# Last rows of a routed mixture of experts: three more blocks of 512 rows, then units of 384, 256 and 128

## The chip, the cores and the metric

The kernel runs on one core of one Trainium2 chip. The metric is the device time of one execution in microseconds (us); the number compared is the median of several executions. One execution is also taken with the hardware profiler, and every row shown below comes from that one. TensorE is called PE, VectorE DVE, ScalarE ACT, GpSimd POOL and SyncE SP; PEld is the loading of weights into PE, and "SPq" or "POOLq" is the sequencer of an engine.

## The reference

A Fourier filter along the sequence gives 19,968 rows of 256 numbers. A gate picks two of eight experts for each row, and the output of a row is the weighted sum of its two experts.

```python
X = np.fft.rfft(x, axis=1)                       # x: 8 x 2496 x 256
x = np.fft.irfft(X * F, n=2496, axis=1).reshape(19968, 256)
noisy = x @ w_gate + np.log1p(np.exp(x @ w_noise)) * noise
top2 = np.argpartition(-noisy, 2, axis=1)[:, :2]  # two of 8 experts
top2_w = softmax over the two
for e in range(8):
    for k in range(2):
        mask = top2[:, k] == e
        h = np.maximum(x[mask] @ w1[e], 0.0)      # 256 -> 1024
        out[mask] += top2_w[mask, k, None] * (h @ w2[e])   # 1024 -> 256
```

So 39,936 rows go through an expert, about 4,990 per expert; which ones is known only once the gate has run.

## The kernel before

The filter is made batch by batch (eight batches), and its matmuls stand among those of the experts. After each batch the gate counts the rows of each expert, writes their numbers into lists in device memory (`route`), and `slots` cuts what has come together into pieces of one size: it makes a small table `tabi` with, for each slot, the place of its list and its expert. The number of slots of a size is fixed when the program is built, since the data can't leave fewer rows than a certain sum: 18 blocks of 512 rows in the first three batches, 23 pairs of two blocks after that, and, when the eighth batch is in, `SINGLE` = 7 single blocks of 512. Then come the remains, `ENDS`: 14 units of 256 rows and 4 of 128. Should the data need more of these (up to 17 and 8), a part behind an `If` at the very end does them one by one. `slots` is called after the last batch for pairs, singles, 256 and 128, in this order; each call is a chain of small DVE instructions with two small matmuls (`sl`, `st`) between them.

All units run through `expert`. A unit of n tiles of 128 rows is handled as follows:

- `read_list` loads its list of row numbers (SP) and turns them into integers (`ids`, POOL).
- `gather` fetches n tiles of rows with indirect DMAs from POOL into the staging slots `xg`, of which there are four of one tile each.
- `turn` brings the rows into the form that PE needs. Blocks of 512 are transposed by DMA (`xt`). Smaller units are copied by POOL (two copies, `kc` = 0 and 1, line 1104 before and 1123 after), transposed by PE (`xps`, one transpose for each tile and kc) and split into a high and a low part (`mxh`, `mxl`).
- `front` loads the two weights of the expert (1 MB each) and splits them, for each unit anew (ACT and DVE, lines 1162 and 1163).
- First layer: 48 matmuls that stream the unit's rows, 128 n columns each (`hps`, lines 123 to 125), into eight results that ACT and DVE take to SBUF (`hh`, `hl`).
- Second layer: for each tile eight pairs of one matmul with 512 columns and one with 256 (`yps`, lines 1235 and 1236). ACT and DVE scale the tile (lines 1240 and 1242), and POOL adds it to the output with an indirect DMA (line 1243, `out<-stage,ids`).

While a unit is in its second layer, the next one has been turned and its first layer is under way. `fetch` sends off the gather of a coming unit; `expert` calls it before the first layer, when

```python
if not self.ahead or self.ahead[0][3] or sum(len(a[2][0]) for a in self.ahead) < 4:
    self.fetch(may)
```

that is, when nothing is waiting, when what waits is turned already, or when fewer than four tiles wait, and again after `front`. Each engine runs its instructions in the order in which the scheduler put them. The tables that say whether the `If` is needed are read into registers of all engines (line 1290): on SP soon after they are made, on the other engines at the end of their work.

## Time and profile before

| | us |
|---|---|
| median of 3 runs (2224.51 to 2234.17) | 2231.22 |
| the profiled execution | 2228.77 |
| its span in the trace | 2227.0 |

The rest of the profiled execution, 1.77 us, lies around the span. In the span PE is busy 98%, DVE 72%, ACT 54% and POOL 45%. By stages: the last single block of 512 rows ends with the DVE instruction at 2015.52 us, the fourteen units of 256 rows follow until about 2183 us, and the four units of 128 rows end at 2217.22 us; the rest of the span is the way of the last tile to device memory and the end of the program. A row of the trace gives a start and a duration; PE's durations overlap, since matmuls are pipelined, so the cost of a matmul is read as the distance between the starts of two of them.

### The profile page before, as it was taken

To read this page: it belongs to the slowest core of one execution; us is meant where nothing else is said; L and a number is where in the kernel's file an instruction comes from. 1 tells how busy PE (TensorE), PEld (TensorE's weight loads), DVE (VectorE), ACT (ScalarE), POOL (GpSimd) and SP (SyncE) were. 2 spreads that over 40 slices of the span, in tenths; PEclk is the share of its full clock that TensorE was granted. 3 is DMA by queue.
4 is the path that set the end of the run, shared out by engine and by line. 5 is a ranking of instruction groups with operands and counts; after the bars stand their busy time and mean duration, and the time that the engine had idled before them with its cause. 6 is when DMAs were issued, how large, how long until landed. Compare 5 with 4: busy or idle time off the path is not lost.

```text
span 2227.0 us, 39429 instructions
## 1 busy us (share of the span) xinstructions
PE 2192.6 (98%) x12687; PEld 1850.7 (83%) x12687; DVE 1613.4 (72%) x3464; ACT 1210.7 (54%) x2373; POOL 1004.9 (45%) x866
## 2 busy tenths in 40 slices
PE   8999999999999999999999999999999999999998
PEld 6668888988888888888888888888888888889997
DVE  4777788869877977787658876696555556567886
ACT  6475655665665455545545454444444444456775
POOL 4035345244433643443444434454545454456663
PEclk9999999999999999999999999999999999999999
DMA  8778879787877767577655767556655556777874
GB/s 248 228 208 220 202 169 213 191 203 174 212 184 176 166 156 178 128 168 167 138 121 129 159 165 138 101 125 125 117 114 120 126 118 140 159 183 222 229 213 123
DMA packets 435434, 370.58 MB, mean 166 GB/s; under 512 B 185643, under 2 KB 345363, under 8 KB 435219
## 3 DMA queue, kind: packets, MB, share of 16 engines
q1 hardware_dynamic: 373907, 283.58, 47.4%
q0 software_dynamic: 61312, 84.40, 23.0%
q8 instruction: 102, 1.67, 0.3%
q14 instruction: 113, 0.93, 0.1%
HBM read 227.73 MB, written 105.25 MB: 150 GB/s over the span
## 4 chain that ended last, share of the span: by engine, by line
PE 93%; DVE 3%; DMA 2%; ACT 1%; issue 1%; SPq 0%; POOL 0%; POOLq 0%; DVEq 0%; ACTq 0%
PE yps L1235 20%; PE hps L123 13%; PE hps L124 13%; PE hps L125 13%; PE yps L1236 10%; PE q L448 3%; PE yps L125 3%; PE yps L124 3%; PE yps L123 3%; PE q L532 2%; DMA stage<-w 1%; PE q L556 1%; PE u L484 1%; PE q L557 1%; PE q L558 1%
## 5 line engine op out<-in xcount | busy, mean ns | idle before, releaser
L1243 POOL DMA_INDIRECT out<-stage,ids x316 | 533.0, 1687 | 363.4 <-DVE stage L1242 199.1
L1235 PE MATMUL yps<-w,hh 128*128 128x512 f32 x1952 | 687.4, 397 | 0.2 <-DVE stage L1242 0.2
L1052 POOL DMA_INDIRECT stage<-y,ids x316 | 343.2, 1086 | 492.3 <-DMA xt<-stage 389.0
L124 PE MATMUL hps<-mxl,w1h 128*128 128x512 f32 (+2 forms) x1424 | 531.3, 374 | 0.3 <-DVE mxl L1116 0.3
L125 PE MATMUL hps<-mxh,w1l 128*128 128x512 f32 (+2 forms) x1424 | 526.3, 371 | 0.0
L1236 PE MATMUL yps<-w,hl 128*128 128x256 f32 x1952 | 520.4, 282 | 0.4 <-DVE hl L1207 0.4
L123 PE MATMUL hps<-mxh,w1h 128*128 128x512 f32 (+2 forms) x1424 | 520.2, 377 | 0.5 <-DVE hl L1207 0.4
L1207 DVE SCALAR_TENSOR_TENSOR hl<-hps,hh 128x512 fp32r<-128x512 f32 (+2 forms) x712 | 433.6, 623 | 90.4 <-ACT hh L1206 88.9
L1206 ACT ACTIVATE hh<-hps 128x512 fp32r<-128x512 f32 (+2 forms) x712 | 379.8, 553 | 196.3 <-PE hps L125 183.7
L1235 PEld LDWEIGHTS yps<-w,hh 128*128 128x128 f32 x1952 | 356.7, 188 | 72.8 <-DVE stage L1242 0.6
L1236 PEld LDWEIGHTS yps<-w,hl 128*128 128x128 f32 x1952 | 367.2, 188 | 27.9 <-DVE hl L1207 1.2
L1240 ACT ACTIVATE stage<-yps,gt 128x256 f32<-128x256 f32 x316 | 142.4, 478 | 366.8 <-PE yps L1236 204.0
L125 PEld LDWEIGHTS hps<-mxh,w1l 128*128 128x128 f32 x1424 | 268.6, 189 | 48.0
L124 PEld LDWEIGHTS hps<-mxl,w1h 128*128 128x128 f32 x1424 | 268.8, 189 | 41.2 <-DVE mxl L1116 1.0
L123 PEld LDWEIGHTS hps<-mxh,w1h 128*128 128x128 f32 x1424 | 264.1, 189 | 43.3 <-DVE hl L1207 3.5
L1242 DVE SCALAR_TENSOR_TENSOR stage<-yps,gt,stage 128x256 f32<-128x256 f32 x244 | 111.9, 479 | 238.0 <-ACT stage L1240 237.7
L1162 ACT CAST w1h<-stage 128x512 fp32r<-128x512 f32 x192 | 119.2, 622 | 120.1 <-DMA stage<-w 59.9
L125 PE MATMUL yps<-w,hl 128*128 128x256 f32 x576 | 159.9, 287 | 2.8 <-DVE hl L1207 2.7
L123 PE MATMUL yps<-w,hh 128*128 128x256 f32 x576 | 161.8, 285 | 0.0
L124 PE MATMUL yps<-w,hh 128*128 128x256 f32 x576 | 161.7, 285 | 0.0
L1163 DVE TENSOR_TENSOR w1l<-stage,w1h 128x512 fp32r<-128x512 f32 x192 | 130.9, 685 | 39.3 <-ACT w1h L1162 38.0
L1163 DVE TENSOR_TENSOR w<-stage,w 128x512 fp32r<-128x512 f32 x228 | 152.5, 683 | 4.8 <-ACT w L1162 4.5
(234 smaller groups left out, 3070.7 us busy)
## 6 DMA issues: line engine op xcount, KB each, us to landing
stage<-w SPq DMA_DIRECT2D x420, 256.0 KB
x<-x SPq DMA_DIRECT2D x88, 256.0 KB
wb<-w SPq DMA_DIRECT2D x18, 1024.0 KB
fx<-fd SPq DMA_DIRECT2D x140, 128.0 KB
fd<-c SPq DMA_DIRECT2D x73, 240.0 KB
out<-z SPq DMA_DIRECT2D x24, 702.0 KB
y<-yt SPq DMA_DIRECT2D x40, 248.6 KB
y<-yt SPq DMA_DIRECT2D x40, 234.0 KB
```

Source lines behind the costliest of these rows:

```text
L123: nc.tensor.matmul(o, lh, rh, start=start, stop=False)
L124: nc.tensor.matmul(o, lh, rl, start=False, stop=False)
L125: return nc.tensor.matmul(o, ll, rh, start=False, stop=stop)
L1052: self.pin(lambda: nc.gpsimd.indirect_dma_start(out=x.bitcast(I32), out_offset=None, in_=self.y[:BLK + ready * ROWS], in_offset=bass.Indir ...
L1162: nc.scalar.copy(h, sv)
L1163: nc.vector.tensor_sub(l, sv, f32v(h))
L1206: r = nc.scalar.activation(h, p, AF.Relu)
L1207: v = nc.vector.scalar_tensor_tensor(l, p, 0.0, f32v(h), op0=ALU.max, op1=ALU.subtract)
L1235: nc.tensor.matmul(bank, h, hl, start=(f == 0), stop=False)
L1236: self.mm = nc.tensor.matmul(p, l, hl[:, 0], start=False, stop=(f == 7))
L1240: nc.scalar.activation(o, p, AF.Copy, scale=gate[:, t])
L1243: a = nc.gpsimd.indirect_dma_start(out=self.io["out"][:BLK + ready * ROWS], out_offset=bass.IndirectOffsetOnAxis(ap=ids[:, t:t + 1], axis= ...
```

## The change

The remains are cut in another way. `SINGLE` is raised by 3, to 10, and a single block may now be filled up: `slots` adds up to 127 rows before it counts. Behind the blocks an expert may have up to seven tiles of 128 left. An odd number of three or more gives one unit of 384 rows (`3 * ROW`) and the rest in units of 256; a single tile gives a unit of 128. `ENDS` now says 3 units of 384, then 5 of 256, and none of 128 in the usual part, and up to 8, 11 and 8 with the part behind the `If`. A unit of 384 is three neighbouring lists of 128. `slots` is called five times after the last batch (pairs, singles, 256, 384, 128), so there is one more table, and the engines read three for the `If`. In the loop, `expert` now fetches ahead only when fewer than three tiles wait, and `gather` goes back to the first of the four staging slots when a unit would run over their end.

```diff
-SINGLE = _sure(LEFT, BLK)
+SINGLE = _sure(LEFT, BLK) + 3
 LEFT -= SINGLE * BLK
-NUNIT = (LEFT + E * (UNIT // 2 - 1)) // UNIT
-USUAL = LEFT // UNIT
-ENDS = (UNIT, USUAL, NUNIT), (UNIT // 2, E // 2, E)
+ROW = 128
+TRIPLE = E // 2 - 1
+USUAL = (LEFT // ROW + E // 2 - 3 * TRIPLE) // 2
+NUNIT = max(E, (LEFT + E * (ROW - 1)) // UNIT)
+ENDS = (3 * ROW, 2, TRIPLE, E), (UNIT, 1, USUAL, NUNIT), (ROW, 3, 0, E)
...
-                    Y += [f(self.gating_more, m // 2)] * 6
+                    Y += [f(self.gating_more, m // 2)] * (8 if n == N else 6)
...
-            todo += [(BLK, SINGLE, True), (UNIT, None, True), (UNIT // 2, None, True)]
+            todo += [(BLK, SINGLE, True, ROW - 1), (UNIT, None, True, ROW - 1), (3 * ROW, None, True, ROW - 1), (ROW, None, True, ROW - 1)]
...
-        v.tensor_scalar_add(ci, cf, float(0 if limit else UNIT // 2 - 1))
-        v.tensor_single_scalar(ci, ci, size.bit_length() - 1, op=ALU.arith_shift_right)
+        v.tensor_scalar_add(ci, cf, float(part))
+        if size >= BLK or size == ROW:
+            v.tensor_single_scalar(ci, ci, size.bit_length() - 1, op=ALU.arith_shift_right)
+        else:
+            v.tensor_single_scalar(ci, ci, ROW.bit_length() - 1, op=ALU.arith_shift_right)
+            v.tensor_copy(cf, ci)
+            if size == 3 * ROW:
+                v.tensor_single_scalar(ci, cf, 2.0, op=ALU.is_gt)
+            else:
+                v.tensor_single_scalar(ci, ci, 1, op=ALU.bitwise_and)
+                v.tensor_copy(new, ci)
+                v.scalar_tensor_tensor(new, cf, 2.0, new, op0=ALU.is_gt, op1=ALU.mult)
+                v.scalar_tensor_tensor(ci, new, -3.0, cf, op0=ALU.mult, op1=ALU.add)
+                v.tensor_single_scalar(ci, ci, 1, op=ALU.arith_shift_right)
...
+        if three:
+            ids, n, nt = ids.rearrange("p n t -> p t n"), 1, 3
...
+        if (self.turns.get("xg", -1) + 1) % 4 + nt > 4:
+            self.turns["xg"] = -1
...
-            if not self.ahead or self.ahead[0][3] or sum(len(a[2][0]) for a in self.ahead) < 4:
+            if not self.ahead or self.ahead[0][3] or sum(len(a[2][0]) for a in self.ahead) < 3:
...
-        with self.tc.If(self.more[0] + self.more[1] < sum(E * CAPB * BLK // u for u, _, _ in ENDS)):
+        with self.tc.If(self.more[0] + self.more[1] + self.more[2] < sum(none(u) for u, _, _, _ in ENDS)):
```

The instructions of every engine stand as before up to the gate of the last batch; from there on three places matter. The first is POOL among the remains. Before, in the run of 256 units (unit 24545 is gathered two units ahead of 23862, whose tiles are still being added to the output):

```order
L1104 COPY stage_83<-stage_83 128x512
L1243 DMA out<-stage_83,ids_23615 21104x256
L1052 DMA stage_83<-y_60,ids_24545 128x264 x2
L1104 COPY stage_83<-stage_83 128x512
L1243 DMA out<-stage_83,ids_23615 21104x256
L1071 ISA
L1071 COPY gt_24709<-stage_83 128x2
L1018 CAST ids_24762<-lt_24760 128x2
```

After, from the first to the third unit of 384 (24440, 24839 and 25099 are their lists, 24142 is that of the last block of 512):

```order
L1123 COPY stage_83<-stage_83 128x768 x2
L1262 DMA out<-stage_83,ids_24142 21104x256
L1090 ISA
L1090 COPY gt_25086<-stage_83 128x3
L1262 DMA out<-stage_83,ids_24142 21104x256 x2
L1071 DMA stage_83<-y_60,ids_25099 128x264 x3
L1262 DMA out<-stage_83,ids_24142 21104x256
L1033 CAST ids_25335<-lt_25333 128x2
L1033 CAST ids_25419<-lt_25417 128x2
L1123 COPY stage_83<-stage_83 128x768
```

The gather of the third unit (25099) now stands behind both copies of the second one and behind its `gt`, since three tiles and three tiles don't fit into four slots; before, a gather stood between the two copies of a unit, with the rows of the one after it.

The second place is the end of PE's work. The last rows of before, in the last unit, which has one tile (27765):

```order
L1235 MATMUL yps_27765<-w2_27762,hh_27747 128x512
L1236 MATMUL yps_27765<-w2_27762,hl_27748 128x256
L1235 MATMUL yps_27765<-w2_27762,hh_27758 128x512
L1236 MATMUL yps_27765<-w2_27762,hl_27759 128x256
L1290 TENSOR_LOAD tabi_18494
L1290 TENSOR_LOAD tabi_18551
```

And of after, in the last unit, which has two (26581 and 26601):

```order
L1254 MATMUL yps_26581<-w2_26578,hh_26574 128x512
L1254 MATMUL yps_26601<-w2_26578,hh_26574 128x512
L1255 MATMUL yps_26581<-w2_26578,hl_26575 128x256
L1255 MATMUL yps_26601<-w2_26578,hl_26575 128x256
L1312 TENSOR_LOAD tabi_18500
```

Both tiles of the last unit are now finished by the last two rows, one right behind the other.

The third place is SP behind the gate of the last batch, where tables are read for the `If`. Before:

```order
L1134 DMA stage_83<-w2 128x512
L1027 TENSOR_LOAD tabi_15675
L1027 ISA x2
L1290 TENSOR_LOAD tabi_18551
L1290 ISA x2
L1134 ISA
L1134 DMA stage_83<-w1 128x512
```

After:

```order
L1044 TENSOR_LOAD tabi_15675
L1044 ISA x2
L1312 TENSOR_LOAD tabi_18559
L1312 ISA x2
L1312 TENSOR_LOAD tabi_18627
L1312 ISA x2
L1153 ISA
L1153 DMA stage_83<-w1 128x512
```

A third table (18627), the last one made, is read ahead of the weights `w1` of the block after next.

## Rows read from the trace of the kernel before

**Rows 1.** The page: busy time and share of each engine; gathers by count and mean.

```profile
PE 2192.6 (98%) x12687; PEld 1850.7 (83%) x12687; DVE 1613.4 (72%) x3464; ACT 1210.7 (54%) x2373; POOL 1004.9 (45%) x866
...
L1052 POOL DMA_INDIRECT stage<-y,ids x316 | 343.2, 1086 | 492.3 <-DMA xt<-stage 389.0
```

**Rows 2.** Stretches, blocks then 256-units: busy PE, PEld, DVE, ACT, POOL; clock, DMA.

```profile
1852.00:2007.00 155.00, 155.00 (x783) 130.72 (x782) 98.13 (x165) 78.52 (x153) 80.19 (x72) 1.00 0.74 171
2027.00:2183.00 156.00, 156.00 (x1096) 143.75 (x1094) 132.68 (x261) 111.74 (x262) 96.66 (x102) 1.00 0.79 221
```

**Rows 3.** What PE waited for from 1500 us to the end: total, times, longest.

```profile
PE yps L1235 <- DVE stage L1242: 0.2, 1, 0.2
```

**Rows 4.** Timeline of DVE, a unit's first finished tile: start, duration, [idle before].

```profile
1854.02 0.87 DVE L1242 SCALAR_TENSOR_TENSOR stage<-yps,gt,stage 128x256 f32<-128x256 f32 x2 [2.35 <-ACT stage L1240]
...
1987.55 0.88 DVE L1242 SCALAR_TENSOR_TENSOR stage<-yps,gt,stage 128x256 f32<-128x256 f32 x2 [2.12 <-ACT stage L1240]
...
2027.15 0.48 DVE L1242 SCALAR_TENSOR_TENSOR stage<-yps,gt,stage 128x256 f32<-128x256 f32 x1 [0.54 <-ACT stage L1240]
...
2182.88 0.48 DVE L1242 SCALAR_TENSOR_TENSOR stage<-yps,gt,stage 128x256 f32<-128x256 f32 x1 [0.72 <-ACT stage L1240]
...
2209.43 0.48 DVE L1242 SCALAR_TENSOR_TENSOR stage<-yps,gt,stage 128x256 f32<-128x256 f32 x1 [0.27 <-ACT stage L1240]
...
2217.22 0.48 DVE L1242 SCALAR_TENSOR_TENSOR stage<-yps,gt,stage 128x256 f32<-128x256 f32 x1 [1.18 <-ACT stage L1240]
```

**Rows 5.** Timeline of PE: starts of first-layer matmuls, 256 columns, then 128.

```profile
2064.24 0.28 PE L123 MATMUL hps<-mxh,w1h 128*128 128x256 f32 x1
...
2065.18 0.28 PE L125 MATMUL hps<-mxh,w1l 128*128 128x256 f32 x1
...
2194.41 0.27 PE L124 MATMUL hps<-mxl,w1h 128*128 128x128 f32 x1
...
2194.86 0.28 PE L125 MATMUL hps<-mxh,w1l 128*128 128x128 f32 x1
```

**Rows 6.** Timeline of PE: two transposes and the matmuls behind them.

```profile
2061.45 0.38 PE L1112 MATMUL xps<-ident,stage 128*128 128x128 f32 x2
...
2061.79 0.28 PE L125 MATMUL hps<-mxh,w1l 128*128 128x256 f32 x1
```

**Rows 7.** POOL's instructions by line, 2020 to 2180 us: duration ns min/median/max.

```profile
L1052 POOL DMA_INDIRECT stage<-y,ids x24: 1009/1030/1084, 2029.8 to 2178.1; - x24
L1104 POOL COPY stage<-stage x27: 656/1005/1262, 2020.3 to 2172.9; 128x512 uint16<-128x512 uint16 x24, 128x256 uint16<-128x256 uint16 x3
L1243 POOL DMA_INDIRECT out<-stage,ids x28: 1580/1603/2023, 2018.8 to 2174.1; - x28
L1071 POOL COPY gt<-stage x14: 766/920/1187, 2022.7 to 2175.1; 128x2 f32 x12, 128x1 f32 x2
L1018 POOL CAST ids<-lt x14: 188/910/923, 2023.4 to 2177.6; 128x2 int32<-128x2 f32 x10, 128x1 int32<-128x1 f32 x4
```

**Rows 8.** The chain that ended last, near its end: an indirect DMA landing.

```profile
2210.19 4.71 DMA out<-stage,ids
```

**Rows 9.** Timeline of the last tile: DVE's row is the last of rows 4.

```profile
2216.71 0.48 ACT L1240 ACTIVATE stage<-yps,gt 128x256 f32<-128x256 f32 x1 [1.00 <-PE yps L1236]
...
2217.97 1.56 POOL L1243 DMA_INDIRECT out<-stage,ids  x1 [5.92 <-DVE stage L1242]
```

**Rows 10.** Tables by line: duration ns, first and last start; SP's waits 1512 to 1560.

```profile
L941 DVE CAST tabi<-tab x3: 172/182/183, 1517.6 to 1532.8; 1x64 int32<-1x64 f32 x3
L1290 SPq TENSOR_LOAD <-tabi x2: 277/444/612, 1525.5 to 1539.3; - x2
L1290 POOLq TENSOR_LOAD <-tabi x2: 291/296/300, 2217.7 to 2218.1; - x2
...
SPq L1134 <- DVE w L1163: 9.3, 3, 8.3
```

More of the change, by code (lines that the diff above doesn't have):

```diff
@@ L885, in gate, with slots @@
         if bt == NB - 1:
-            todo += [(BLK, SINGLE, True), (UNIT, None, True), (UNIT // 2, None, True)]
+            todo += [(BLK, SINGLE, True, ROW - 1), (UNIT, None, True, ROW - 1), (3 * ROW, None, True, ROW - 1), (ROW, None, True, ROW - 1)]
         for a in todo:
             yield from self.slots(*a)
-    def slots(self, size, limit, fresh):
+    def slots(self, size, limit, fresh, part=0):
         nc, P, v = self.nc, self.P, self.nc.vector
@@ L897, in slots @@
         ci, cf, new, st, en = t("ci", dt=I32), t("cf"), t("new"), t("st"), t("en")
[L898 removed]
+        gran = ROW if size == 3 * ROW else min(size, BLK)
         k = size // gran
         v.tensor_sub(cf, self.cnt, self.done)
[L901 to L902 removed]
+        v.tensor_scalar_add(ci, cf, float(part))
[12 more added lines that the diff above has]
+                v.tensor_single_scalar(ci, ci, 1, op=ALU.arith_shift_right)
         v.tensor_copy(new, ci)
@@ L938, in slots @@
         v.tensor_add(self.tab, self.tab, q[:1, 16:16 + 2 * SW].rearrange("p (a b) -> p a b", a=2))
-        tabi = P.tile([1, 2, SW], I32, name="tabi", bufs=6)
+        tabi = P.tile([1, 2, SW], I32, name="tabi", bufs=7)
         self.tabs.append(tabi)
@@ L1005, in read_list @@
         nc = self.nc
-        gran = min(size, BLK)
+        three = size == 3 * ROW
+        gran = ROW if three else min(size, BLK)
         n, nt, none = size // gran, gran // 128, E * CAPB * BLK // gran
@@ L1254, in run, with none @@
         state = {"ready": -1, "n": 0, "c": 0}
+        def none(u):
+            return E * CAPB * BLK // (ROW if u == 3 * ROW else u)
         def step():
@@ L1289, in parts @@
                 yield from cut(self.read_list(NB, s, BLK), NB)
-            self.more = [self.nc.values_load(self.tabs[NB + 1 + i][0:1, 0, n:n + 1], min_val=0, max_val=E * CAPB * BLK // u)
-                         for i, (u, n, _) in enumerate(ENDS)]
-            for i, (u, n, _) in enumerate(ENDS):
+            self.more = [self.nc.values_load(self.tabs[NB + i][0:1, 0, n:n + 1], min_val=0, max_val=none(u)) for u, i, n, _ in ENDS]
+            for u, i, n, _ in ENDS:
                 for s in range(n):
-                    yield from cut(self.read_list(NB + 1 + i, s, u), NB)
+                    yield from cut(self.read_list(NB + i, s, u), NB)
         def may():
@@ L1312, in run @@
                 pass
-        with self.tc.If(self.more[0] + self.more[1] < sum(E * CAPB * BLK // u for u, _, _ in ENDS)):
+        with self.tc.If(self.more[0] + self.more[1] + self.more[2] < sum(none(u) for u, _, _, _ in ENDS)):
             self.sp = self.spw = None
-            rest = (((*self.read_list(NB + 1 + i, s, u), NB), 0) for i, (u, a, b) in enumerate(ENDS) for s in range(a, b))
+            rest = (((*self.read_list(NB + i, s, u), NB), 0) for u, i, a, b in ENDS for s in range(a, b))
             for _ in self.expert(rest, lambda: True):
```

1 line of the change is left out of this document (removed).

## Prediction

> **What bounds the kernel now.** I read the shares first, then the stretches, then PE's waits. PE is busy 98% of the span [rows 1]. A busy PE alone proves little, because its durations overlap, so the second look is at the place that changes: among the last single blocks and among the 256-row units PE is busy for the whole stretch, at a granted clock of 1.00 (2.4 GHz), while DVE has 98.13 of 155 us in the first and 132.68 of 156 in the second [rows 2]. From 1500 us to the end PE waited once, for 0.2 us [rows 3]. So the tail is bound by what PE is given to do, and the question is how many PE microseconds the rows of the remains cost in each size of unit. DVE is the nearest follower, and nearest with 256-row units (85%), since each unit splits 2 MB of weights whatever its size.
>
> **Price of a unit.** Units follow each other at a steady distance, read from the DVE instruction that finishes a unit's first tile [rows 4]. Seven blocks of 512 lie between 1854.02 and 1987.55, six distances: 22.26 us each. Fourteen 256-row units from 2027.15 to 2182.88, thirteen distances: 11.98. From there three 128-row units to 2209.43: 26.55 in all, 8.85 each; the last one comes 7.79 later, since no unit behind it shares PE. Per tile that is 5.6, 6.0 and 8.9 us: the small units are dear.
>
> The 384-row unit is in no row, so I build it from PE's instructions. A block has 48 matmuls of 512 columns and 32 pairs of 512 and 256; if 256 columns cost half, that is 96 matmuls of 512, so 22.26 / 96 = 0.232 us each and 0.348 a pair. First-layer matmuls of 256 columns start 0.94 / 8 = 0.1175 us apart, those of 128 columns 0.45 / 4 = 0.1125 [rows 5]: from 256 down to 128 nothing is saved, which is why the 128-row unit is dear. Two transposes and one matmul of 256 columns take 0.34 us [rows 6], so a transpose 0.11. The sum for a 256-row unit is 48 x 0.1175 + 16 x 0.348 + 4 x 0.11 = 11.65, 0.33 under the measured 11.98; for a 128-row unit it is 5.40 + 2.78 + 0.22 = 8.40, 0.45 under 8.85. So each small unit has some 0.38 us that no instruction fills. For 384 columns I take the middle of 0.1175 and 0.232, 0.175: 48 x 0.175 + 24 x 0.348 + 6 x 0.11 + 0.38 = **17.8 us**. Bounds: the middle of 11.98 and 22.26, 17.1; and 20.5, if a matmul of 384 columns cost as much as one of 512.
>
> The Trainium skill (TensorE: Matmul & The Clock Gate, "Back-to-back issue gap") gives the isolated distance of matmuls as N / 2.4 + 2.5 ns, 162.5 for 384 columns; an estimate with it makes the unit 17.2 us and the gain below 1.8 us larger. By the same formula 512 columns would take 216 ns where this trace has 232, so I stay with the rows.
>
> **The change part by part.**
>
> *Fewer and larger units.* Before, the trace has 316 gathered tiles [rows 1] = 18 x 4 + 46 x 4 + 7 x 4 + 14 x 2 + 4, so the part behind the If did not run. Now there are 10 blocks, 3 x 384 and 5 x 256: 315 tiles. Removed: 14 x 11.98 + 26.55 + 7.79 = 202.1. Added: 3 x 22.26 = 66.8; 3 x 17.8 = 53.4; four 256-row units, 47.9; and a last one with nobody behind it, which I shorten as the last 128-row unit was (7.79 for 8.85): 11.98 - 1.06 = 10.9. Sum 179.0, so **-23.1 us**. All of it is on the path, because PE is. The weights loaded shrink from 25 to 18 times 2 MB, and DVE falls from its 85%; neither is worth anything here, as PE does not wait for them.
>
> *The end.* The last tile goes ACT at 2216.71, DVE at 2217.22, POOL's add at 2217.97 [rows 4, 9]. Now two tiles finish within one matmul of each other, and POOL adds them one after the other at 1.60 us each [rows 7], so the end is **+1.6** later. A third table is read by each engine at the end; POOL's reads take 0.3 us and stand around the last add [rows 10]: **+0.3**, between 0 and 1.2 (four engines in turn).
>
> *The longer gate chain.* One more call of `slots` and some extra steps: about 33 small DVE instructions and three small matmuls. On PE I take **+0.5** for the matmuls and their places. The rest is hidden if it delays nothing. The three tables were finished from 1517.6 to 1532.8, so 7.6 us apart; a fourth comes at about 1540.4. SP read its second one at 1539.3 and now reads a third right behind it [rows 10], so SP stands still for 1 to 2 us, at most 7.6. Behind it are the weights of a coming block. They wait for DVE's splits to clear their slots in any case (9.3 us in this stretch, once 8.3 [rows 10]), and that cover hides the read; without it PE would lose up to 7.6.
>
> *Fetching ahead at fewer than three waiting tiles.* For blocks (4 tiles) and 256-row units (2) the condition decides as before. It bites only on 384-row units, and is free as long as a gather has time, see the second rival.
>
> Sum: -23.1 + 1.6 + 0.3 + 0.5 = **-20.7 us**. The profiled execution of 2228.77 (its span of 2227.0 and 1.77 around it) becomes 2208.1; the median lies 2.45 higher, at 2231.22, and becomes **2210.5 us** (0.9% less).
>
> **The rivals.**
>
> *Thin gain.* The 384-row unit costs 20.5 us, by the rate of 512 columns or because ACT and DVE can't keep up with its eight results. Three units lose 3 x 2.7 = 8.1: 2218.6. Against it: DVE has 63% with blocks and 85% with 256-row units [rows 2], and 384 lies between.
>
> *The gather comes late: slower than before.* Two 384-row units don't fit into the four staging slots, so the gather of the next waits until POOL has copied the one before it, and POOL does things in order. Take the second and third 384-row units. In POOL's order stand, from the second copy of the one to the first copy of the other: a copy (1.26, the largest row), an add, `gt` (0.92), two adds, three gathers, the landing (4.7, bounded by the landing of an add [rows 8]; another add and two casts run under it) and a copy: 1.26 + 1.6 + 0.92 + 3.2 + 3.1 + 4.7 + 1.26 = 16.0 us [rows 7, 8]. The chain can begin when PE has made the first unit's second transposes, which frees the buffer of that copy, and must be done when PE comes to the third unit's first ones. In PE's order 58 first-layer matmuls of 384 columns, 32 pairs and 6 transposes lie between: 10.15 + 11.14 + 0.66 = 22.0 us by the prices above. So 6 us are to spare, and the chain is hidden. Should the adds in it be held up by that much and more, PE loses time at three handovers (to the second and third 384-row unit and to the first 256-row one); the gain is gone at 20.7 / 3 = 6.9 us lost at each. With the whole chain of 16.0 us in the open at all three it is 48.0 - 20.7 = +27.3: 2258.5. For it: POOL's adds wait for DVE. Against it: POOL is busy for 96.66 of 156 us [rows 2], and a 384-row unit gives it about 50% more work in 50% more time.
>
> The Trainium skill speaks against the change here: "Double-buffer for performance: Overlap DMA with compute" (Trainium Kernel Development and Optimization, "Best Practices"), and 384-row units give up the second buffer of the gather. By that rule the handovers would show as gaps on PE; no row of before can show it, since every pair of small units there fits into the slots.
>
> *The If runs: the change does not do what it says.* Counting the reference's own rows per expert, the remains after the blocks are 336, 347, 378, 249 and 962 rows (the other three experts end in a filled-up block), which is 3 x 384, 1 + 4 x 256 and nothing else: it fits, but 378 and 249 are only 6 and 7 rows below the next size. One unit more behind the If would run alone: two landings (9.4), its gathers and copies, both layers and its adds unhidden, some 30 us; 2240.
>
> **How the numbers follow.** The forecast has 0.78, thin gain 0.09, late gathers 0.08 (half of them with most of the 16 us), the gate's chain or SP at up to 7.6 us more 0.03, the If 0.02. Half a per cent, about what a measurement of this kernel can tell from no change, is 11.2 us: faster means below 2220.1, slower above 2242.4. Faster: the forecast, two thirds of the thin gain, 0.02 of the gate's and 0.01 of the late gathers, 0.87. Within half a per cent: the rest of the thin gain and of the gate's, 0.03 of the late gathers, and the If at 2240, 0.09. Slower: the other half of the late gathers, 0.04. The range: with 17.1 for the unit (-2.1) and no cost at the end (-2.4) it is 2206, and the runs of before scatter by 3 to 7 us to either side of their median, so 2203; upwards the thin gain at 2218.6 is taken in: 2219. Left out are the late gathers, the If and the far ends of the others, 0.15 in all.
>
> **What would show it.** In the trace after, the finished tiles should stand 22.3 us apart for ten blocks, 17 to 18.5 for 384-row units and 12.0 for 256; PE should have no wait over 1 us between 1500 us and its last matmul; 315 gathers; two adds of 1.6 us back to back at the end. A PE wait at the transposes of a 384-row unit means late gathers; a wait at its first-layer results means thin gain; a wait for weights near 1545 us means SP; more than 315 gathers mean that the If ran. The prediction is wrong at its root if PE is no longer busy throughout the tail.

## The result, and the profile after

The changed kernel takes **2204.95 us**, the median of 4 runs (2203.32 to 2207.78), against 2230.89 for the kernel before in the same comparison (4 runs, 2224.51 to 2234.17). The ratio is 0.9896, with a 95% interval of 0.9882 to 0.991: 23.2 us less, between 20.1 and 26.3 (the two medians lie 25.9 us apart). Forecast were 2210.5 us in a range of 2203 to 2219, and 20.7 us less. It became faster by more than half a per cent, as forecast, and the gain is at the large end of what I had worked out.

The profiled execution of after took 2203.32 us, with a span of 2201.3. Its page, busy time and share of each engine, then the gathers:

```profile
PE 2165.6 (98%) x12315; PEld 1821.5 (83%) x12315; DVE 1569.0 (71%) x3372; ACT 1169.2 (53%) x2246; POOL 992.0 (45%) x830
...
L1071 POOL DMA_INDIRECT stage<-y,ids x315 | 343.0, 1089 | 491.8 <-DMA xt<-stage 384.3
```

Against [rows 1] PE has the same 98% and 27.0 us less to do. There are 315 gathers, one fewer: the part behind the If did not run. The stretches of the last blocks, the 384-row units and the 256-row units (columns as in [rows 2]: start and end, length, then busy time of PE, PEld, DVE, ACT and POOL, PE's granted clock, DMA share, GB/s):

```profile
1851.00:2051.00 200.00, 200.00 (x1009) 168.59 (x1008) 128.77 (x216) 101.66 (x199) 104.86 (x91) 1.00 0.74 164
2074.00:2126.00 52.00, 52.00 (x304) 48.47 (x303) 33.84 (x61) 29.88 (x61) 34.65 (x35) 1.00 0.64 165
2143.00:2190.00 47.00, 46.00 (x321) 42.24 (x319) 34.67 (x71) 29.40 (x71) 19.52 (x16) 1.00 0.44 104
```

PE is busy for all of the first two and granted full clock (2.4 GHz) in all three; the idle microsecond of the third is the wait below and the half microsecond behind PE's last matmul (2189.07 + 0.40 us). DVE is at 65% with 384-row units. What PE waited for from 1500 us to the end, as in [rows 3]:

```profile
PE hps L125 <- DVE hl L1226: 0.5, 1, 0.5
```

One wait, of half a microsecond. Nothing took the place of the units that are gone. The finished first tiles (DVE's timeline, columns as in [rows 4]): one at 1500 us, the mark at the start of the tail, the one nine blocks later, the last block, three 384-row units and five 256-row units:

```profile
1497.68 0.47 DVE L1261 SCALAR_TENSOR_TENSOR stage<-yps,gt,stage 128x256 f32<-128x256 f32 x1
...
1851.12 0.88 DVE L1261 SCALAR_TENSOR_TENSOR stage<-yps,gt,stage 128x256 f32<-128x256 f32 x2 [2.35 <-ACT stage L1259]
...
2051.38 0.88 DVE L1261 SCALAR_TENSOR_TENSOR stage<-yps,gt,stage 128x256 f32<-128x256 f32 x2 [1.58 <-ACT stage L1259]
...
2072.27 0.88 DVE L1261 SCALAR_TENSOR_TENSOR stage<-yps,gt,stage 128x256 f32<-128x256 f32 x2 [1.10 <-ACT stage L1259]
...
2093.32 0.88 DVE L1261 SCALAR_TENSOR_TENSOR stage<-yps,gt,stage 128x256 f32<-128x256 f32 x2 [0.42 <-ACT stage L1259]
...
2110.84 0.88 DVE L1261 SCALAR_TENSOR_TENSOR stage<-yps,gt,stage 128x256 f32<-128x256 f32 x2 [0.43 <-ACT stage L1259]
...
2127.95 0.88 DVE L1261 SCALAR_TENSOR_TENSOR stage<-yps,gt,stage 128x256 f32<-128x256 f32 x2 [0.54 <-ACT stage L1259]
...
2142.51 0.88 DVE L1261 SCALAR_TENSOR_TENSOR stage<-yps,gt,stage 128x256 f32<-128x256 f32 x2 [0.55 <-ACT stage L1259]
...
2178.86 0.88 DVE L1261 SCALAR_TENSOR_TENSOR stage<-yps,gt,stage 128x256 f32<-128x256 f32 x2 [0.55 <-ACT stage L1259]
...
2189.94 0.88 DVE L1261 SCALAR_TENSOR_TENSOR stage<-yps,gt,stage 128x256 f32<-128x256 f32 x2 [3.54 <-ACT stage L1259]
```

The blocks stand (2051.38 - 1851.12) / 9 = 22.25 us apart, the 384-row units 17.52 and 17.11, the 256-row units from 2142.51 to 2178.86 three distances of 12.1 on the mean (12.01, 12.40 and 11.94; the half-microsecond wait lies in the second), and the last one comes 11.08 later. The end, POOL's two last adds:

```profile
2190.70 1.55 POOL L1262 DMA_INDIRECT out<-stage,ids  x1 [7.66 <-DVE stage L1261]
2192.55 1.55 POOL L1262 DMA_INDIRECT out<-stage,ids  x1 [0.30 <-issue]
```

They stand 1.85 us apart, where before had one [rows 9].

**Where the 25.7 us of the two spans come from** (2227.0 - 2201.3). I cut both traces at a mark that both have, the finished tile near 1850 us (1854.02 in [rows 4], 1851.12 here), and at the one near 1500 us. The row of before for the latter:

```profile
1501.06 0.47 DVE L1242 SCALAR_TENSOR_TENSOR stage<-yps,gt,stage 128x256 f32<-128x256 f32 x1
```

- Up to the mark near 1500: after is 1501.06 - 1497.68 = 3.4 us ahead, where the change moves nothing on PE's path. Experiment 2 has a larger shift there between two executions of one order.
- From there to the mark near 1850: 352.96 before, 353.44 after, +0.5. The longer gate chain lies here (experiment 2 has it alone).
- From the mark to the end, "the tail" in what follows: 2227.0 - 1854.02 = 372.98 before, 2201.3 - 1851.12 = 350.18 after, **-22.8**. Of it -24.4 lies between the mark and the last unit's (363.20 and 338.82), and +1.6 behind the last unit's mark (9.78 and 11.36).

### The profile page after: what moved, and what is told of

Same layout as the page of the kernel before. It is cut to its first block, busy times and chain, and to the rows that moved or that the text cites. A ratio compares the mean times of both kernels' runs of the same rounds, so it can differ in the third digit from the quotient of the medians.

```text
span 2201.3 us, 38091 instructions
## 1 busy us (share of the span) xinstructions
PE 2165.6 (98%) x12315; PEld 1821.5 (83%) x12315; DVE 1569.0 (71%) x3372; ACT 1169.2 (53%) x2246; POOL 992.0 (45%) x830
## 4 chain that ended last, share of the span: by engine, by line
PE 90%; DVE 4%; ACT 2%; DMA 2%; issue 1%; SPq 0%; POOL 0%; another core or an unknown queue 0%; ACTq 0%; POOLq 0%; DVEq 0%
PE yps L1254 20%; PE hps L126 13%; PE hps L125 13%; PE hps L127 12%; PE yps L1255 10%; PE q L450 3%; PE yps L127 3%; PE yps L125 3%; PE yps L126 3%; PE q L534 2%; DMA stage<-w 1%; PE q L558 1%; PE u L486 1%; PE q L559 1%; PE q L560 1%
## 5 line engine op out<-in xcount | busy, mean ns | idle before, releaser
L1262 POOL DMA_INDIRECT out<-stage,ids x315 | 543.5, 1725 | 360.6 <-DVE stage L1261 180.1
L126 PE MATMUL hps<-mxl,w1h 128*128 128x512 f32 (+2 forms) x1312 | 508.3, 388 | 0.3 <-DVE mxl L1135 0.3
L127 PE MATMUL hps<-mxh,w1l 128*128 128x512 f32 (+2 forms) x1312 | 503.9, 385 | 0.0
L125 PE MATMUL hps<-mxh,w1h 128*128 128x512 f32 (+2 forms) x1312 | 495.9, 389 | 1.1 <-DVE hl L1226 1.0
L1226 DVE SCALAR_TENSOR_TENSOR hl<-hps,hh 128x512 fp32r<-128x512 f32 (+2 forms) x656 | 425.8, 663 | 94.0 <-ACT hh L1225 87.6
L1225 ACT ACTIVATE hh<-hps 128x512 fp32r<-128x512 f32 (+2 forms) x656 | 371.1, 584 | 193.3 <-PE hps L127 174.6
L127 PEld LDWEIGHTS hps<-mxh,w1l 128*128 128x128 f32 x1312 | 246.8, 188 | 50.0
L126 PEld LDWEIGHTS hps<-mxl,w1h 128*128 128x128 f32 x1312 | 247.1, 188 | 42.2 <-DVE mxl L1135 1.0
L125 PEld LDWEIGHTS hps<-mxh,w1h 128*128 128x128 f32 x1312 | 243.6, 188 | 41.9 <-DVE hl L1226 3.0
L1182 DVE TENSOR_TENSOR w1l<-stage,w1h 128x512 fp32r<-128x512 f32 x204 | 139.5, 689 | 37.9 <-ACT w1h L1181 27.1
L126 PE MATMUL yps<-w,hh 128*128 128x256 f32 x576 | 161.6, 285 | 0.0
```

The source lines that it names most:

```text
L125: nc.tensor.matmul(o, lh, rh, start=start, stop=False)
L126: nc.tensor.matmul(o, lh, rl, start=False, stop=False)
L127: return nc.tensor.matmul(o, ll, rh, start=False, stop=stop)
L1182: nc.vector.tensor_sub(l, sv, f32v(h))
L1225: r = nc.scalar.activation(h, p, AF.Relu)
L1226: v = nc.vector.scalar_tensor_tensor(l, p, 0.0, f32v(h), op0=ALU.max, op1=ALU.subtract)
```

## The experiments

The theory: PE is the bound, a unit costs what its matmuls cost, and the two parts of the change (three more blocks; units of 384) add up. The rivals: the gather behind 384-row units is nearly late, so that some of the gain is already lost there; the gate chain costs more than it shows; DVE sets the distance of the small units. Tails are compared, since they leave out the early part, in which executions differ; ratios where runs were repeated. The kernel before had medians of 2225.16, 2224.73 and 2232.0 us in the three comparisons that follow, so times aren't compared across them.

**1. The two halves of the change.** In the first kernel only the three blocks are added to the kernel before; the second is the changed kernel without them.

```diff
-SINGLE = _sure(LEFT, BLK)
+SINGLE = _sure(LEFT, BLK) + 3
...
-        v.tensor_scalar_add(ci, cf, float(0 if limit else UNIT // 2 - 1))
+        v.tensor_scalar_add(ci, cf, float(0 if limit and not (size == BLK and limit == SINGLE and fresh) else UNIT // 2 - 1))
```

> Before, with the three more (filled-up) blocks of 512 alone; what is left goes in 8 units of 256 and 4 of 128, no unit of 384. Theory (PE bound, steady prices of the rows): six units of 256 go, 6 x 11.98 = 71.9 us, three blocks come, 3 x 22.24 = 66.7, so 5.2 us faster than before, the end as before (one last tile). Rival (larger units pay through DVE and the weights, not only through PE's own sum): seven units of weights saved become eight, and the gain is clearly above 5, towards 10. If blocks brought most of the whole change, it would be 15 or more.

```diff
-SINGLE = _sure(LEFT, BLK) + 3
+SINGLE = _sure(LEFT, BLK)
...
-            todo += [(BLK, SINGLE, True, ROW - 1), (UNIT, None, True, ROW - 1), (3 * ROW, None, True, ROW - 1), (ROW, None, True, ROW - 1)]
+            todo += [(BLK, SINGLE, True), (UNIT, None, True, ROW - 1), (3 * ROW, None, True, ROW - 1), (ROW, None, True, ROW - 1)]
```

> The changed kernel with the 7 blocks of before: the units of 384 alone. What is left is 3 units of 384 and 11 of 256, no 128. Theory: against before, three units of 256 (35.9 us) and four of 128 (34.3) go, three of 384 come. At 17.4 us each, as the trace after has them, 52.2, plus 1.6 at the end, 0.5 for the gate's chain and less 1 for the last unit: about 17 us faster. At the 17.8 of the prediction 16 us faster. Thin gain (20.5 each) would leave 8. Blocks and 384-row units should add up: this and the blocks alone make some 22.

Measured: the blocks alone 2218.35 against 2225.16, ratio 0.997 (0.9957 to 0.9982); the units alone 2209.16, ratio 0.9927 (0.9911 to 0.9944). The marks of the two, from DVE's timeline:

```profile
1849.28 0.88 DVE L1242 SCALAR_TENSOR_TENSOR stage<-yps,gt,stage 128x256 f32<-128x256 f32 x2 [2.35 <-ACT stage L1240]
```

```profile
1851.79 0.88 DVE L1261 SCALAR_TENSOR_TENSOR stage<-yps,gt,stage 128x256 f32<-128x256 f32 x2 [2.35 <-ACT stage L1259]
```

With spans of 2217.0 and 2207.4 the tails are 367.72 and 355.61: -5.3 and -17.4 against 372.98. Together -22.7, and the whole change has -22.8. The parts add up, and the blocks are what their own units cost: three for six 256-row units are 3 x 22.26 - 6 x 11.98 = -5.1. The -17.4 of the units holds their price and the handover from the blocks to them, which the section on why takes apart.

**2. The kernel before with the same order, and the gate chain alone.** The first kernel only takes over the new condition and one more table buffer, which changes nothing in the order of any engine (the instructions of PE, DVE, ACT and POOL stand in the same order in both traces); the second adds the longer chain, a fourth table that holds nothing and the third read.

```diff
-        tabi = P.tile([1, 2, SW], I32, name="tabi", bufs=6)
+        tabi = P.tile([1, 2, SW], I32, name="tabi", bufs=7)
...
-            if not self.ahead or self.ahead[0][3] or sum(len(a[2][0]) for a in self.ahead) < 4:
+            if not self.ahead or self.ahead[0][3] or sum(len(a[2][0]) for a in self.ahead) < 3:
```

> Before, with the condition of fewer than three waiting tiles and one more buffer for the tables, and nothing else; the instructions of every engine stand in the same order as before. Theory: no difference, within 0.2%. The profile after was 3.8 us ahead of that of before already at 744 us, where both run the same instructions in the same order; if that is chance of a run, this kernel's profile may show either value (a wait of 4 us of PE near 193 us or none) and its median lies on that of before. If the memory layout does it, all kernels with the seventh buffer are 3 to 4 us faster than before.

```diff
-                    Y += [f(self.gating_more, m // 2)] * 6
+                    Y += [f(self.gating_more, m // 2)] * (8 if n == N else 6)
...
-            todo += [(BLK, SINGLE, True), (UNIT, None, True), (UNIT // 2, None, True)]
+            todo += [(BLK, SINGLE, True), (UNIT, None, True), (UNIT // 2, None, True), (UNIT // 2, None, True)]
...
+            self.more += [self.nc.values_load(self.tabs[NB + 3][0:1, 0, 0:1], min_val=0, max_val=E * CAPB * BLK // (UNIT // 2))]
```

> Before, with a further call of slots after the last batch (it finds no rows left), eight steps of the chain and a third table read for the If. Theory: 0.5 us on PE near 1510 to 1550 us and 0.3 at the end, 0 to 2 us slower in all, within the noise. Rival: SP stands at the third table and the weights of a coming block come late: up to 7.6 us slower, with a wait of PE near 1545 us.

Measured: ratios 0.9995 (0.9986 to 1.0005) and 1.0001 (0.9991 to 1.0012), with ten runs each. The marks near 1850 of the one and the other:

```profile
1848.08 0.88 DVE L1242 SCALAR_TENSOR_TENSOR stage<-yps,gt,stage 128x256 f32<-128x256 f32 x2 [2.35 <-ACT stage L1240]
```

```profile
1848.32 0.88 DVE L1242 SCALAR_TENSOR_TENSOR stage<-yps,gt,stage 128x256 f32<-128x256 f32 x2 [2.35 <-ACT stage L1240]
```

The first stands 5.9 us ahead of the same mark in [rows 4], in a kernel that does the same things in the same order, and its tail of 2221.0 - 1848.08 = 372.92 is that of before. So some 6 us come and go in the early part, and the 3.4 us by which the profile of after is ahead there is no gain of the change. One place where such time goes is a wait of PE near 193 us, 4.0 us in before's profile and 1.7 in this kernel's; its row here (total, times, longest):

```profile
PE q L339 <- ACT c L380: 1.7, 1, 1.7
```

With the gate chain the mark near 1500 is

```profile
1494.87 0.47 DVE L1242 SCALAR_TENSOR_TENSOR stage<-yps,gt,stage 128x256 f32<-128x256 f32 x1
```

so from there to the mark near 1850 it is 1848.32 - 1494.87 = 353.45 us, where before has 352.96 and after 353.44: the chain alone costs the 0.5 us that after shows. The tail is 2221.6 - 1848.32 = 373.28, so it costs at most a few tenths there. No wait of PE over 0.2 us follows after 1500 us: SP's standing still behind the third table, for which I had kept up to 7.6 us, isn't seen.

**3. How near to late is the gather?** Ahead of the first gather of each 384-row unit POOL clears its buffer 12 or 36 times, which changes no result and delays POOL.

```diff
             x = self.slot("xg")
+            for _ in range(12 if nt == 3 and t == 0 else 0):
+                nc.gpsimd.memset(x, 0.0)
```

> The changed kernel with 12 vain memsets of 0.3 us, 3.6 us in all, on POOL ahead of the gather of each unit of 384. Asked: how much room the gather has at a handover, since two such units don't fit into the staging slots. By the prediction 6 us are to spare, so the tail (from the first tile of the block that is finished near 1850 us to the end of the span, 350.2 us in the trace after) stays within 1 us. If the room were what the trace after shows between POOL's last copy and PE's transposes of the third unit (the copy ends at 2091.08, the transposes start at 2091.47, 0.4 us), it would be some 3 us longer at each of three handovers, 359.

The second kernel has 36 in place of 12.

> The same with 36 memsets, 10.8 us, at each gather of a unit of 384. With 6 us to spare, some 5 us are lost at each of three handovers: the tail 365. With 0.4 us to spare, 10 us each: 381. If the transposes are placed by when the rows can be there and are not themselves urgent, the room is larger and the tail stays near 350.

Measured (one execution each): with 12 the stretch from the last block's mark to the end is 2201.7 - 2069.07 = 132.63 us, where after has 2201.3 - 2072.27 = 129.03: +3.6. With 36 it is 2216.8 - 2073.19 = 143.61: +14.6. Here are POOL's first copy of the third 384-row unit in after and two of PE's transposes there, the second ones of the second unit and the first ones of the third (a unit is transposed twice, for `kc` = 0 and 1; x3 are the three tiles of a 384-row unit, x2 the two of a 256-row unit):

```profile
2089.98 1.10 POOL L1123 COPY stage<-stage 128x768 uint16<-128x768 uint16 x1
...
2091.31 0.49 PE L1131 MATMUL xps<-ident,stage 128*128 128x128 f32 x3
...
2094.25 0.49 PE L1131 MATMUL xps<-ident,stage 128*128 128x128 f32 x3
```

The kernel with 12 clears: POOL's group of the clears between 2010 and 2120 us (form and count, busy us, mean ns, idle before), then PE's same two transposes and the first ones of the 256-row unit behind:

```profile
L1072 POOL MEMSET stage<- 128x264 f32 x36 | 14.0, 389 | 2.8 <-DMA xt<-stage 1.1
```

```profile
2088.71 0.49 PE L1133 MATMUL xps<-ident,stage 128*128 128x128 f32 x3
...
2098.77 0.55 PE L1133 MATMUL xps<-ident,stage 128*128 128x128 f32 x3 [0.97 <-POOL stage L1125]
...
2112.26 0.44 PE L1133 MATMUL xps<-ident,stage 128*128 128x128 f32 x2 [1.78 <-POOL stage L1125]
```

The kernel with 36: the clears between 2020 and 2160 us, and the transposes of PE that waited, the first ones of the second and of the third unit:

```profile
L1072 POOL MEMSET stage<- 128x264 f32 x108 | 42.9, 397 | 6.0 <-DMA xt<-stage 0.9
```

```profile
2090.64 0.90 PE L1133 MATMUL xps<-ident,stage 128*128 128x128 f32 x3 [6.82 <-POOL stage L1125]
...
2124.34 0.55 PE L1133 MATMUL xps<-ident,stage 128*128 128x128 f32 x3 [1.67 <-POOL stage L1125]
```

PE waits where the rival said it would, at the transposes, for POOL's copies. With 12 clears it waits at the handovers to the third 384-row unit and to the first 256-row unit, whose gather has no clears of its own but stands behind the third unit's on POOL; with 36 it waits at those to the second and the third. (The expectations count three handovers; two bear it each time.) The clears put in 14.0 / 3 = 4.7 and 42.9 / 3 = 14.3 us at each unit. What of it stays hidden is no measure of after's own margin, though: with the clears the scheduler makes another order. In after the third unit's first transposes start 2.94 us behind the second unit's second ones, with 12 clears 10.06 us, and 0.97 of that is the wait, so some 6 us of PE's other work were put between them. The margin of after stands in its own rows: POOL's copy ends at 2091.08, and PE's transposes of the third unit start at 2094.25, so 3.2 us are to spare there, not 6. (The 0.4 us of the expectation takes the second unit's transposes for the third's.) What matters is that after has a margin and doesn't wait.

The larger delay costs more than its wait. The first two stretches from mark to mark in the kernel with 36, then short stretches around the wait (columns as in the stretches above):

```profile
2073.19:2102.73 29.54, 22.72 (x124) 20.77 (x123) 12.53 (x23) 10.98 (x24) 24.91 (x48) 0.88 0.60 165
2102.73:2119.05 16.32, 15.85 (x91) 14.55 (x89) 10.30 (x19) 9.27 (x20) 13.29 (x28) 1.00 0.49 132
```

```profile
2087.00:2090.64 3.64, 0.00 (x0) 0.00 (x1) 0.00 (x0) 0.00 (x0) 3.15 (x4) 0.51 0.36 58
2090.64:2092.00 1.36, 1.36 (x6) 1.36 (x7) 0.00 (x0) 0.00 (x0) 1.21 (x3) 0.50 0.37 56
2092.00:2094.00 2.00, 2.00 (x8) 1.90 (x7) 0.17 (x1) 0.82 (x2) 1.87 (x4) 0.53 0.13 7
2094.00:2096.00 2.00, 2.00 (x14) 1.87 (x13) 1.45 (x3) 0.57 (x2) 1.66 (x2) 1.00 0.43 58
```

PE stood idle for 6.8 us up to 2090.64. In that time its granted clock fell to 0.51, and it worked on at that level (1.2 GHz) until 2094. The same 124 matmuls that take 21.05 us in after took 22.72, so the late gather cost 6.8 of waiting and 1.7 of slow matmuls. (The second stretch has 91 instructions of PE, and the same one in after 104: here too the order is another.)

**4. A second buffer for the gather.** The 384-row units gather into a region that is free by then, three tiles twice, and the rows may again be fetched ahead while fewer than four tiles wait. Once so, and once with the 36 clears.

```diff
+        if nt == 3:
+            self.turns["x3"] = 3 - self.turns.get("x3", 3)
-        if (self.turns.get("xg", -1) + 1) % 4 + nt > 4:
+        elif (self.turns.get("xg", -1) + 1) % 4 + nt > 4:
...
-            x = self.slot("xg")
+            x = self.triples(self.turns["x3"] + t, 1) if nt == 3 else self.slot("xg")
...
-            if not self.ahead or self.ahead[0][3] or sum(len(a[2][0]) for a in self.ahead) < 3:
+            if not self.ahead or self.ahead[0][3] or sum(len(a[2][0]) for a in self.ahead) < 4:
```

> The changed kernel with two staging buffers of three tiles of their own for the units of 384 (in the filter's place, which is free by then), fetched ahead at fewer than four waiting tiles. In the trace after PE waits for no gather, so the theory gives no difference: the tail 350 +/- 1. If the single buffer costs something that the waits don't show, the tail is 1 to 4 us shorter.

> The same two buffers, and the 36 memsets on POOL for the gather of each unit of 384 that made the tail 14.6 us longer with one buffer. Theory (what costs there is that the gather can't begin before the unit ahead of it has been copied): the memsets find their place earlier and the tail comes back to within 3 us of 350. Rival (POOL has no 10.8 us to give, whatever the buffers): it stays 10 us or more longer.

Measured (one execution each): without clears 2209.1 - 2079.70 = 129.40 us from the last block's mark to the end, with 36 clears 2214.3 - 2083.91 = 130.39, against 129.03 for after. PE's wait in the latter:

```profile
PE xps L1140 <- POOL stage L1132: 1.2, 1, 1.2
```

So the second buffer, with the earlier fetch that it allows, is worth nothing here, and with a slow POOL it would be worth 14.6 - 1.4 = 13.2 us. The Trainium skill (Trainium Kernel Development and Optimization, "Best Practices") says to double-buffer so that transfers overlap compute; these two runs agree where POOL is late, and the changed kernel shows when the rule needn't be paid for: its gather has time enough between the copies out of the one buffer and the next transposes. The old condition with 384-row units and four slots wasn't tried.

**5. Does DVE set the distance of the 256-row units?** DVE's splitting of the weights is cut in the 256-row units: in the first kernel the low parts of w1 aren't made (the high parts stand for them), in the second neither those nor the low parts of w2 (which POOL clears to zero). The second one's edit, in part:

```diff
+        if high and nm == "w1":
+            return h, h
+        if high:
+            nc.gpsimd.memset(f32v(l), 0.0)
+            return hl
...
-                w1.append(self.wsplit(w1st[q], "w1", q))
+                w1.append(self.wsplit(w1st[q], "w1", q, nt == 2))
```

> The changed kernel without the low parts of w1 in the units of 256 rows (the high parts stand in their place in the third matmul of the first layer, so PE does as much): DVE has four splits of 0.69 us less in each of these units. Asked: what leaves 0.33 us empty in a unit of 256 and nothing in a unit of 384. Theory (DVE, 85% busy with 256-row units and 65% with 384): the distance of 256-row units goes from 12.0 to some 11.7. Rival (turning PE from one kind of work to another costs it, whoever waits): it stays at 12.0.

> The changed kernel without the low parts of both weights in the units of 256 rows (for w1 the high part stands in, for w2 POOL writes zeros), so that DVE has eight splits of 0.69 us less in each of these units. Leaving out four brought the distance from 12.1 to 11.86 us. If DVE makes the rest of the gap too, it comes to the sum of PE's instructions, 11.65; if the rest is PE's own cost of changing between kinds of work, it stays at 11.86. POOL's zeros may disturb it.

Measured (one execution each), the first and last marks of 256-row units in the first kernel:

```profile
2140.13 0.88 DVE L1263 SCALAR_TENSOR_TENSOR stage<-yps,gt,stage 128x256 f32<-128x256 f32 x2
...
2175.71 0.88 DVE L1263 SCALAR_TENSOR_TENSOR stage<-yps,gt,stage 128x256 f32<-128x256 f32 x2
```

Three distances of 11.86; in the second kernel, with still less for DVE, 11.85, 11.86 and 11.84. Before had 11.98 and after 12.1. So the splits that DVE no longer makes cost between 0.1 and 0.25 us in such a unit, and 0.2 over PE's own sum of 11.65 stay.

The traces show where this time lies. In before's 256-row units it is in the first layer, where one matmul starts late and the next one too. The rows of PE at this place, then DVE's, which takes two first-layer results out (`hl`):

```profile
2065.89 0.28 PE L125 MATMUL hps<-mxh,w1l 128*128 128x256 f32 x1
2066.13 0.39 PE L123 MATMUL hps<-mxh,w1h 128*128 128x256 f32 x1
2066.35 0.28 PE L124 MATMUL hps<-mxl,w1h 128*128 128x256 f32 x1
```

```profile
2065.66 0.75 DVE L1207 SCALAR_TENSOR_TENSOR hl<-hps,hh 128x256 fp32r<-128x256 f32 x2
```

The starts are 0.24 and 0.22 us apart where 0.12 is usual. One `hl` takes 0.42, so the first of the two ends at 2066.08, and PE goes on 0.05 later: PE is held until DVE has emptied a result. The list of waits doesn't show it, since a matmul's row of 0.28 us reaches over a hold this short. The same place holds after's one listed wait. With four splits less for DVE the hold is gone there. What stays of the 0.2 is for the most part, 0.14, a like hold at another place: in the first kernel L126 starts at 2151.97, just behind DVE's `mxl` (2151.49 and 0.42 long), and the next matmul 0.23 later.

**6. Other arrangements.** The 384-row units behind the 256-row ones, so that the last unit has three tiles, of which one ends by itself; and two more blocks still.

```diff
-ENDS = (3 * ROW, 2, TRIPLE, E), (UNIT, 1, USUAL, NUNIT), (ROW, 3, 0, E)
+ENDS = (UNIT, 1, USUAL, NUNIT), (3 * ROW, 2, TRIPLE, E), (ROW, 3, 0, E)
...
-            if not self.ahead or self.ahead[0][3] or sum(len(a[2][0]) for a in self.ahead) < 3:
+            if not self.ahead or self.ahead[0][3] or sum(len(a[2][0]) for a in self.ahead) < (3 if self.pairs < USUAL else 1):
```

> The changed kernel with the units in the other order: five of 256, then three of 384 (fetched ahead only when nothing waits once the units of 256 have all been fetched). The last unit then ends with one tile by itself, not two at once. Theory: the end after the last tile's first mark is 9.8 us as before and not 11.4, so 1.6 us faster than the changed kernel, 24.8 instead of 23.2 us faster than before. Rival: the first 384-row unit, which can't be fetched while a 256-row unit waits, is late, and this costs up to 10 us.

```diff
-SINGLE = _sure(LEFT, BLK) + 3
+SINGLE = _sure(LEFT, BLK) + 5
```

> The changed kernel with 12 single blocks in place of 10 (SINGLE + 5): the 962 rows of the last expert go in two blocks, the second filled up, and not in four units of 256; what is left is 3 units of 384 and 1 of 256. Theory: four units of 256 go at 12.0, two blocks come at 22.24, the tail 3.5 us shorter than the 350.2 of the changed kernel, so some 26.7 us faster than before (ratio 0.988). Rival: the units of 384 stand right before the end, and what their late gathers or the last unit cost is no longer covered: no gain.

Measured: 384 last gives 2204.75 against 2224.73, ratio 0.9912 (0.9895 to 0.9928), and 2201.0 - 2069.87 = 131.13 us from the last block's mark to the end, +2.1 against after where I had expected a gain. The marks of the last block and of the first 256-row unit, and PE's two waits that after doesn't have:

```profile
2069.87 0.88 DVE L1263 SCALAR_TENSOR_TENSOR stage<-yps,gt,stage 128x256 f32<-128x256 f32 x2 [1.06 <-ACT stage L1261]
...
2088.78 0.88 DVE L1263 SCALAR_TENSOR_TENSOR stage<-yps,gt,stage 128x256 f32<-128x256 f32 x2 [0.54 <-ACT stage L1261]
```

```profile
PE yps L1256 <- DVE stage L1263: 1.2, 2, 1.0
```

The blocks here hand over to a 256-row unit again, and that takes 18.91 us, as in before (18.88), 1.2 of them empty, where after's handover to a 384-row unit has 0.15 empty (the section on why has the sums). One of the two waits, 0.2 us, is part of this; the other, 1.0 us, comes at the last unit. Together that is the +2.1. The saving at the end didn't come: the last add stands alone, but starts 10.3 us ahead of the span's end, where after's second starts 8.75 ahead and before's one 9.03. In this execution the very last landing of an add comes at 2196.06, 1.2 us behind the one ahead of it, while in before the last sixteen lie within 0.3 us. So this run doesn't settle what two adds at the end cost.

Twelve blocks give 2203.19 against 2232.0, ratio 0.9883 (0.9863 to 0.9904), and the tail by this mark

```profile
1851.82 0.88 DVE L1261 SCALAR_TENSOR_TENSOR stage<-yps,gt,stage 128x256 f32<-128x256 f32 x2 [2.35 <-ACT stage L1259]
```

is 2198.6 - 1851.82 = 346.78, 3.4 us shorter than after's. Two blocks for four 256-row units are 2 x 22.25 - 4 x 11.98 = -3.4: the same arithmetic once more. By the times alone it can't be told from after, whose interval of 0.9882 to 0.991 overlaps.

## Why the prediction was right, step by step

**PE bounds the tail.** Right: busy throughout, one wait of 0.5 us after 1500 us, and the two halves of the change add up to a tenth of a microsecond (experiment 1). The exception is small: in a 256-row unit PE is held by DVE for some 0.3 of 12 us, under busy rows (experiment 5).

**Fewer and larger units, -23.1.** Measured -24.4 between the mark and the last unit's, 1.3 more. The blocks came as forecast (22.25 for 22.26). The mis-sized term is the **384-row unit, 17.8**: the first two of them lie 17.52 apart. The step that failed is the 0.38 us "that no instruction fills", which I carried over from the small units: PE's own sum without it is 48 x 0.175 + 24 x 0.348 + 6 x 0.11 = 17.41, and the unit leaves 0.1 empty. In the 256-row unit the gap is PE's hold behind DVE (experiment 5), no cost that every unit has. Three times 0.28 is 0.8 of the 1.3. (The next distance, 17.11, is no price: between those marks PE does 41 first-layer matmuls of 384 columns and already 9 of the 256-row unit behind.)

A second term was left out, the handover from the blocks to the small units. The mark of before's last block is

```profile
2008.27 0.88 DVE L1242 SCALAR_TENSOR_TENSOR stage<-yps,gt,stage 128x256 f32<-128x256 f32 x2 [1.06 <-ACT stage L1240]
```

and that of the first 256-row unit 2027.15 [rows 4], 18.88 us later. PE does 52 first-layer matmuls of 256 columns, 32 pairs and 4 transposes between them, 52 x 0.1175 + 32 x 0.348 + 4 x 0.11 = 17.69, so 1.2 us are empty: the wait of 0.2 us for DVE [rows 3], and holds behind DVE as in experiment 5. After has 2093.32 - 2072.27 = 21.05 for 52 of 384 columns, 32 pairs and 6 transposes, 20.90: 0.15 empty, 1.0 less. Against this the 256-row units came at 12.1 for 11.98 and the last one at 11.08 for 10.9, together 0.6 dearer. In all -0.84 - 1.04 + 0.58 = -1.3.

The other part of the 384-row unit's price, a matmul of 384 columns in the middle of those of 256 and 512, held. Two starts on PE, 18 matmuls apart:

```profile
2080.26 0.34 PE L127 MATMUL hps<-mxh,w1l 128*128 128x384 f32 x1
...
2083.41 0.34 PE L127 MATMUL hps<-mxh,w1l 128*128 128x384 f32 x1
```

3.15 / 18 = 0.175 us. The estimate of 162.5 ns by the formula of the Trainium skill (TensorE: Matmul & The Clock Gate, "Back-to-back issue gap") was 7% low, as it is for the 512 columns that I had held against it.

**The end, +1.6 and +0.3.** Measured +1.6 behind the last unit's mark for both together. The two adds stand back to back, 1.85 us apart, and the last one's start lies 8.75 us ahead of the span's end where before had 9.03; so the third table's read adds nothing that shows. That the second add makes the 1.6 fits these rows, but no run shows it alone (experiment 6). SP's and POOL's reads of the three tables, by line (duration ns min/median/max, first and last start):

```profile
L1312 SPq TENSOR_LOAD <-tabi x3: 263/277/431, 1522.1 to 1536.8; - x3
...
L1312 POOLq TENSOR_LOAD <-tabi x3: 284/288/296, 2190.9 to 2191.7; - x3
```

POOL's stand between the starts of the two adds, in the shadow of the first.

**The gate chain, +0.5.** Measured +0.5 between 1500 and 1850 us, in after and alone (experiment 2), too small for the ratio there to show (1.0001). SP's wait behind it didn't come: its three reads (the row above) take 0.26 to 0.43 us each, and PE waited for no weights.

**The sum.** -24.4 + 1.6 + 0.5 = -22.3 where -20.7 was forecast: 1.3 us from the units and the handover and 0.3 from the end make the difference. With -22.3 the median would be 2208.9. The other 4 us down to 2204.95 lie outside what the change does, as far as the rows show it. The runs of one kernel scatter by some 5 us to either side, the profiles differ by 3.4 us in a part that the change doesn't touch, and experiment 2 shows 5.9 us there without any change. Without the 3 us that the range had for this scatter its lower bound was 2206, and the median would have missed it: that the number lies inside is in part luck.

**The rivals.** *Thin gain* is refuted by the row of 0.175 us and by DVE's 65%. *Late gather*: its place and mechanism are real (experiment 3: the wait comes exactly at the transposes, and experiment 4: with a second buffer 8.5 us of it shrink to 1.2), but its condition isn't met. The margin at the third unit is 3.2 us and not the 6 that I had worked out. PE's side of the sum held: its transposes at 2071.80 and 2094.25, between which it lay, are 22.45 us apart for 22.0. POOL's chain took 14.2 us for 16.0, but its first copy began only at 2076.85, 5.0 us behind the transposes that the forecast let it begin with. So this was the rival nearest to coming true, nearer than I thought; had it come, its price could have been higher than its waits, as in the run where PE's clock fell in a wait of 6.8 us. *The If* didn't run: 315 gathers. *SP* wasn't held up.

## What to carry to other kernels

Where one engine is busy throughout, price a new unit size by that engine's own instructions alone, at their measured distances, and check the price by doing each half of the change alone; a gap seen in smaller units need not come along, and the handover from one size to the next has a price of its own. Before giving up a second buffer, add up what must happen between the last use of the one buffer and the next need, and read the margin from the trace; a run with that chain delayed on purpose shows where the wait would come, but its order can be another. A difference between two profiles counts only if it lies where the change is: cut both at a mark that both have.

## What the runs showed of the hardware

- At the low clock level a stream of these matmuls took nearly twice as long. PE's timeline with 36 clears, just behind the wait of 6.8 us:

```profile
2091.98 0.52 PE L127 MATMUL hps<-mxh,w1l 128*128 128x384 f32 x1
...
2092.94 0.52 PE L127 MATMUL hps<-mxh,w1l 128*128 128x384 f32 x1
```

  Three matmuls later, 0.96 / 3 = 0.32 us each at a granted clock of 0.50 to 0.53, where after has 0.175 at 1.00. The 0.32 is N / 1.2 GHz, which the Trainium skill (TensorE: Matmul & The Clock Gate, "Back-to-back issue gap") gives for that level; the rows at the high level have 0.175, where its formula gives 0.1625.
- The distance of first-layer matmuls is 0.1125, 0.1175, 0.175 and 0.232 us for 128, 256, 384 and 512 columns (the first two [rows 5], the last worked out from [rows 4]): from 256 on it grows by some 0.057 per 128 columns, and below 256 hardly at all.
- Two executions of the same order (experiment 2 and the profile of before) differ by 5.9 us in the first 1850 us, and by under 0.1 us in the 373 behind them.
